# Retention attention and two MoE layers: the decay mask made on the chip, and a new order of the first loads

## Chip, cores and metric

The kernel runs on one core of a Trainium2 chip. The metric is the device time of one launch in microseconds (us), taken as the median of several runs. A profile is one execution more, with its own time. Five engines take part: PE (TensorE, matmuls), DVE (VectorE), ACT (ScalarE), SP (SyncE, which here only issues DMAs) and POOL (GpSimd, idle but for four constants at the start). PEld is the loading of weights into PE, which overlaps its matmuls.

## What is computed

```python
# attention: B, H, S, D = 2, 8, 768, 64
gamma = 1.0 - 2.0 ** (-5.0 - np.arange(H))
scale = 1.0 / np.sqrt(D)
for t in range(S):
    state = gamma * state + outer(k[:, :, t], v[:, :, t])
    y[:, :, t] = scale * (q[:, :, t] @ state)
# x = y as 1536 tokens x 512
h = x @ w_in;  x = (h * clip(h + 3, 0, 6) / 6) @ w_out        # layer 0, d_ff 2048
h = x @ w_in2; out = (h * tanh(softplus(h))) @ w_out2         # layer 1, d_ff 2048
```

Everything is float32 in and out. Matmuls of the two layers split each operand into a high and a low float32r part and take three passes (high by high, low by high, high by low).

## The kernel before

The attention is done in 12 units: six chunks of 128 positions for each of two batches; unit u is chunk u // 2 of batch u % 2. For a unit the names below are these. `qk` and `kv` are its two loads (512 and 516 KB). `sc` is the scores matmul (eight small fp32 matmuls, into one `wx` and one `wy` bank of PSUM). `m` are the two DVE multiplications of the scores by `mask`, which give `A` (L533). `kp` are eight ACT scalings of k (L524). `kv` on PE adds k by v to the running state in the bank `acc0` or `acc1` (L540 on), and `st` is ACT's copy of that state (L545). `qs` is DVE's scaling of q by a table, `qtab` (L529), in all units but the first two. `pv` is the output: `qs` by the state, then `A` by v. From its bank ACT writes `xh` (L580) and two quarters `q`/`qc` (L589), and DVE writes `xl` (L583). These are the inputs of layer 0.

Before the units, DVE zeroes a tile (L377) and PE multiplies zero by zero into `acc0` and `acc1` (`run_warm`, L380), which clears the two banks of the states. That is four fp32 matmuls of 256 columns.

The mask is a table of 128 by 1024 float32 (eight heads by 128 positions, for each of 128 key positions): the decay gamma to the power of the distance, times the scale, and zero above the diagonal. It is computed on the host and loaded as the third of the loads (L254).

The layers' weights come as `raw` words in 64 bits, of which ACT and DVE make float32 (`cvu`, `cvd`: L414 to L424) and then high and low parts (`wbh`, `wbl`, `tv`, `wdh`, `wdl`: L431, L433). An up-product `h` of layer 0 is 12 passes of 512 columns; `o` are the passes of the down-products.

The order of all this is made when the program is built. Every step is a task with an engine, an assumed duration and a rank, and `Plan.order` places the task that can start first, the lower rank first among equals. Ranks of the PE tasks of the beginning follow the string `EARLY`: s is `sc`, k is `kv`, b is `pv`, h is an up-product, o a down-product. The first loads are ranked by `LOADS`; what is not named there follows. `GATE` gives how long the up-products of the second layer are held back behind the first layer's last down-products. Each engine then runs its list in order, and so does SP's queue of DMAs. A load waits for its buffer (three each for `qk` and `kv`, two for `raw` and for `qtab`), and from the ninth on for the load issued eight places ahead of it to have landed, since eight semaphores serve the DMAs in turn.

Of the kernel before, what the change touches and what calls it, by code (L numbers as in the profile page):

```python
# [12 lines left out]
F32R = mybir.dt.float32r  # L13
# [3 lines left out]
ALU = mybir.AluOpType  # L17
PSUM = bass.MemoryType.PSUM

B, H, S, D = 2, 8, 768, 64  # L20
P = 128
# [4 lines left out]
NPAIR = H // 2  # L26
# [13 lines left out]
DMA512 = 1.28  # L40
MMR = 0.2266
MMH = 0.12
DVE1 = 0.686
# [3 lines left out]
SC, KV, PV = 0.9, 0.47, (0.9, 1.8)  # L47
TURN = 0.17
LEAD = (7.2, 6.1)
GATE = {'c': 8.0, 'w': 8.5, 'v': 8.0}  # L50
EARLY = "ssbsksbkskkbkksbbhkskbsbbksbokhoshbhshhoosbohohbohoohhhooo"
LOADS = "qk0 kv0 mask qk1 qk2 kv1 kv2 t1 kv3 qk3"
DLAT = 1.45
OUT = 4.0


# [27 lines left out]
class Plan:  # L84
# [3 lines left out]
    def add(self, nm, eng, dur, deps, bufs, emit, rank=None):  # L88
        t = Task(nm, eng, dur, deps, bufs, emit, rank)
        t.idx = len(self.tasks)  # L90
        self.tasks.append(t)
        for b in bufs:
            if not b.users:
                t.new.append(b)
                b.owner = t
            elif b.owner not in t.deps:
                t.deps.append(b.owner)
            b.users.append(t)
        for d in t.deps:
# [84 lines left out]
def body(ctx: ExitStack, tc: tile.TileContext, aps: dict, out: bass.AP):  # L184
# [39 lines left out]
    def wk(kind=None):  # L224
        if kind is None:
            turn[0] += 1
            kind = "xy"[turn[0] % 2]
        return buf("wk", [P, 512], "w" + kind)

    mask_b = buf("att", [P, 1024], "mask")  # L230
    qtab_b = {c: buf("att", [P, 512], "qtab") for c in range(1, NCH)}

    def load(nm, b, src, us, rank=None):
        return add(nm, "SP", us, [], [b],
                   lambda: nc.sync.dma_start(out=b.tile, in_=src), rank)  # L235
# [6 lines left out]
    def ld(u, what, rank=None):  # L242
        if what == "qk":
            ld_qk[u] = load(f"qk{u}", qk[u], aps["qk"][u], DMA512, rank=rank)
        else:
            ld_kv[u] = load(f"kv{u}", kv[u], aps["kv"][u], DMA512, rank=rank)

    tabs = aps["tabs"]
    lds = {}
    for n, what in enumerate(LOADS.split() + [f"{x}{u}" for u in range(NU) for x in ("qk", "kv")]  # L250
                             + [f"t{c}" for c in range(1, NCH)]):
        rank = -100 + n if n < len(LOADS.split()) else None
        if what == "mask":
            lds[what] = load("mask", mask_b, aps["mask"], DMA512, rank=rank)  # L254
        elif what[0] == "t":
            if what not in lds:
                c = int(what[1:])
                lds[what] = load(f"qtab{c}", qtab_b[c], tabs[:, (c - 1) * 512:c * 512], DMA512 / 2, rank=rank)
        elif what not in lds:
            ld(int(what[2:]), what[:2], rank)  # L260
            lds[what] = True
    ld_mask = lds["mask"]


    flow = []
# [40 lines left out]
    def source(i):  # L306
        layer, g, b, f = downs[i]
        if plain[layer, g]:
            return ("c", layer, f, b)
        if b == 0:  # L310
            return ("v", layer, f // 2, 4 if f % 2 else 3)
        return ("w", layer, f // 2, {(1, 0): 2, (1, 1): 4, (2, 0): 3, (2, 1): 7}[b, f % 2])
# [33 lines left out]
    hq = i = 0  # L346
    for c in EARLY:
        if c in "skb":
# [9 lines left out]
    while i < ND or hq < len(ups):  # L358
        nxt = ups[hq] if hq < len(ups) else None
        gate = 0.0  # L360
        if nxt and nxt[1] == 1:
            gate = max((done_at.get(b, 1e9) + GATE[nxt[0]]) for b in ((1, 2) if nxt[0] == "w" else (0,)))
        ready = up_end.get(source(i), 1e9) + LEAD[downs[i][0]] if i < ND else 1e9
# [9 lines left out]
            clock[0] = max(clock[0] + 0.05, min(ready, gate if nxt else 1e9))  # L373

    att_tasks = []
    zb = buf("fix", [P, 512], "t")
    z0 = add("zero", "DVE", DVE1, [], [zb], lambda: V.memset(zb.tile, 0.0), -99)  # L377
    kv_acc = [buf("acc", [P, 512], f"acc{b}") for b in range(B)]

    def run_warm():  # L380
        for a in kv_acc:
            for n in range(2):
                mm(a.tile[:, n * 256:n * 256 + 256], zb.tile[:, 0:P], zb.tile[:, 0:256], n == 0, True)
    t_warm = add("warm", "PE", 1.8, [z0], [zb] + kv_acc, run_warm, -99)

    wbase, wquart, wsum, wdown = {}, {}, {}, {}
    ld_w = [None]

# [113 lines left out]
    def unit(u):  # L502
        c, b = divmod(u, B)
# [4 lines left out]
        ps = [wk(), wk()]  # L508
# [6 lines left out]
        t_sc = add(f"sc{u}", "PE", SC, [ld_qk[u], pvs.get(u - BUFS["A"])], [qb] + ps, sc, pe_rank["sc", u])  # L515
# [11 lines left out]
        if c > 0:  # L527
            qsb = buf("att", [P, DM], "qs")
            t_qs = add(f"qs{u}", "DVE", DVE1, [ld_qk[u], lds[f"t{c}"]], [qb, qsb, qtab_b[c]], lambda: V.tensor_tensor(  # L529
                out=qsb.tile, in0=qb.tile[:, 0:512], in1=qtab_b[c].tile, op=ALU.mult))  # L530
        ab = buf("att", [P, 2, 512], "A")
        t_m = [add(f"m{u}_{i}", "DVE", DVE1, [t_sc, ld_mask], [ps[i], ab, mask_b],
                   lambda i=i: V.tensor_tensor(out=ab.tile[:, i, :], in0=ps[i].tile,  # L533
                                               in1=mask_b.tile[:, i * 512:(i + 1) * 512], op=ALU.mult))
               for i in range(2)]
# [39 lines left out]

        out_rank = pe_rank["pv", u] + PV[u >= B] + OUT

        def p3():
# [5 lines left out]
                                          op=ALU.subtract), out_rank + 0.7)  # L584
# [8 lines left out]
    for u in range(NU):  # L593
        unit(u)
# [295 lines left out]
def _tables():  # L890
    h = np.arange(H, dtype=np.float64)
    gam = 1.0 - 2.0 ** (-5.0 - h)
    scale = 1.0 / math.sqrt(D)
    i = np.arange(P)
    dif = i[None, :] - i[:, None]
    m = np.where(dif[:, None, :] >= 0, gam[None, :, None] ** np.maximum(dif, 0)[:, None, :], 0.0) * scale
    mask = m.reshape(P, NPAIR, 2, P).transpose(0, 2, 1, 3).reshape(P, 1024)
    gp = gam.reshape(NPAIR, 2)
    qt = [np.repeat((scale * gp[:, :, None] ** (c * P + i)).transpose(1, 0, 2)[:, None], 64, axis=1).reshape(P, 512)
          for c in range(1, NCH)]  # L900
    ktab = np.stack([gam[None, :] ** (-(u // B * P + i[:, None]).astype(np.float64)) for u in range(NU)])
    return mask.astype(np.float32), np.concatenate(qt, 1).astype(np.float32), ktab.astype(np.float32)


def _lay_w(w_in, w_out):
# [33 lines left out]
```

## Time and profile before

| | |
|---|---|
| median of 3 runs | 556.09 us (555.86 to 556.11) |
| the profiled execution, its own time | 556.31 us |
| its span, first to last recorded event | 554.5 us |
| PE busy | 544.5 us |
| DVE busy | 421.3 us |
| ACT busy | 289.7 us |
| bytes read and written by DMA | 51.2 MB |

The span is what the profile covers; 1.8 us of the execution lie around it. Busy time of PE includes the modelled ends of its matmuls, so short holes do not show in it. Busy shares are means over stages that have different limits: the first 25 us, in which the loads arrive one behind another, are not like the rest.

### The profile page before, as it was taken

The page shows a single profiled execution, that of the slowest core. Times are in us where ns is not written, and L with a number is a line of the kernel's source. Part 1 is how long each engine was busy: PE and PEld are TensorE (multiplying, and loading weights), DVE is VectorE, ACT ScalarE, POOL GpSimd, SP SyncE. Part 2 cuts the span into 40 slices and gives each one's busy share as a digit, 9 for nine tenths or more (in the row PEclk, how much of TensorE's full clock was granted, in tenths as well). Part 3 has the DMA queues.
Part 4 walks back from the last instruction along what each step waited for, and adds up shares of the span by engine and source line. Part 5 has one row for each costly group of instructions (what it writes and reads, how often), then busy time and mean ns, then how long its engine had stood idle before and what let it go on. Part 6 is the DMA issues. An engine that isn't in the chain of part 4 may idle for free.

```text
span 554.5 us, 8001 instructions
## 1 busy us (share of the span) xinstructions
PE 544.5 (98%) x3184; PEld 463.7 (84%) x3184; DVE 421.3 (76%) x651; ACT 289.7 (52%) x553; POOL 0.2 (0%) x4
## 2 busy tenths in 40 slices
PE   7899999999999999999999999999999999999997
PEld 6798888888889988888898888888888888988875
DVE  3799997599956996679999999899327985763243
ACT  4998645585625643455537665645433553442430
POOL 0000000000000000000000000000000000000000
PEclk9999999999999999999999999999999999999999
DMA  8986424003220233001222024224200240001003
GB/s 334 407 346 267 152 77 141 12 10 143 76 77 0 77 93 137 0 8 69 77 77 76 2 76 152 76 77 152 76 1 0 77 151 2 0 1 54 23 28 125
DMA packets 10981, 51.68 MB, mean 93 GB/s; under 512 B 1216, under 2 KB 1216, under 8 KB 7104
## 3 DMA queue, kind: packets, MB, share of 16 engines
q1 hardware_dynamic: 10944, 51.17, 25.8%
q8 instruction: 25, 0.41, 0.3%
q14 instruction: 12, 0.10, 0.1%
HBM read 48.02 MB, written 3.15 MB: 92 GB/s over the span
## 4 chain that ended last, share of the span: by engine, by line
PE 95%; DMA 3%; DVE 1%; SPq 0%; issue 0%
PE acc L216 51%; PE wx L216 24%; PE wy L216 20%; DMA qk<-in_qk_dram 3%; DVE sb L834 0%; SPq L235 0%; DVE g L745 0%
## 5 line engine op out<-in xcount | busy, mean ns | idle before, releaser
L216 PE MATMUL acc<-gh,wdh 128*128 128x512 f32 x192 | 74.9, 390 | 0.0
L216 PE MATMUL acc<-gh,wdl 128*128 128x512 f32 x192 | 74.8, 390 | 0.0
L216 PE MATMUL acc<-wdl,gh 128*128 128x512 f32 x192 | 74.8, 390 | 0.0
L216 PE MATMUL acc<-wdh,gh 128*128 128x512 f32 x192 | 74.8, 390 | 0.0
L216 PE MATMUL acc<-wdh,gl 128*128 128x512 f32 x192 | 74.7, 389 | 0.0
L216 PE MATMUL acc<-gl,wdh 128*128 128x512 f32 x192 | 74.7, 389 | 0.0
L781 DVE TENSOR_TENSOR gl<-g,gh 128x512 fp32r<-128x512 f32 x68 | 46.7, 687 | 25.7 <-ACT gh L779 21.1
L779 ACT CAST gh<-g 128x512 fp32r<-128x512 f32 x68 | 42.2, 621 | 30.3 <-PE acc L216 18.2
L745 DVE TENSOR_TENSOR g<-wy,g 128x256 f32<-128x256 f32 (+1 forms) x42 | 21.4, 509 | 28.6 <-PE wy L216 28.4
L216 PEld LDWEIGHTS acc<-gl,wdh 128*128 128x128 f32 x192 | 36.0, 188 | 7.6
L216 PEld LDWEIGHTS acc<-wdh,gl 128*128 128x128 f32 x192 | 36.0, 188 | 7.5
L216 PEld LDWEIGHTS acc<-gh,wdh 128*128 128x128 f32 x192 | 36.1, 188 | 7.3 <-issue 0.2
L216 PEld LDWEIGHTS acc<-wdh,gh 128*128 128x128 f32 x192 | 36.1, 188 | 7.2
L216 PEld LDWEIGHTS acc<-wdl,gh 128*128 128x128 f32 x192 | 36.1, 188 | 7.2
L216 PEld LDWEIGHTS acc<-gh,wdl 128*128 128x128 f32 x192 | 36.1, 188 | 7.0
L781 DVE TENSOR_TENSOR gl<-gs,gh 128x512 fp32r<-128x512 f32 x28 | 19.3, 688 | 22.7 <-ACT gh L779 16.9
L779 ACT CAST gh<-gs 128x512 fp32r<-128x512 f32 x28 | 17.4, 622 | 31.0 <-PE acc L216 30.9
L431 ACT CAST wdh<-cvd 128x512 fp32r<-128x512 f32 x32 | 19.7, 620 | 20.6 <-PE acc L216 16.3
L433 DVE TENSOR_TENSOR wdl<-cvd,wdh 128x512 fp32r<-128x512 f32 x32 | 21.9, 686 | 10.9 <-ACT wdh L431 10.5
L742 ACT COPY g<-wx 128x256 f32<-128x256 f32 (+1 forms) x42 | 18.5, 441 | 21.2 <-PE wx L216 20.9
L834 DVE SCALAR_TENSOR_TENSOR sb<-acc,sb 128x512 f32<-128x512 f32 x36 | 23.3, 685 | 4.5 <-PE acc L216 4.5
L431 ACT CAST wsh<-cvu 128x1024 fp32r<-128x1024 f32 x14 | 14.7, 1051 | 21.1 <-DVE cvu L477 21.0
(191 smaller groups left out, 1339.9 us busy)
## 6 DMA issues: line engine op xcount, KB each, us to landing
raw<-in_w_dram SPq DMA_DIRECT2D x30, 1024.0 KB, 4.8
kv<-in_kv_dram SPq DMA_DIRECT2D x12, 516.0 KB, 6.9
qk<-in_qk_dram SPq DMA_DIRECT2D x12, 512.0 KB, 7.4
out_dram<-sb SPq DMA_DIRECT2D x12, 256.0 KB, 2.1
raw<-in_w_dram SPq DMA_DIRECT2D x4, 512.0 KB, 10.0
qtab<-in_tabs_dram SPq DMA_DIRECT2D x5, 256.0 KB, 8.1
mask<-in_mask_dram SPq DMA_DIRECT2D x1, 512.0 KB, 6.1
```

The costliest lines, as they stand in the source:

```text
L216: nc.tensor.matmul(o, l, r, start=start, stop=stop, skip_group_check=True)
L431: lambda: A.copy(hb.tile[:, h0:h0 + n], cb.tile[:, c0:c0 + n]))
L433: return add(nm + "lo", "DVE", dve(n), [a], list(dict.fromkeys([cb, hb, lb])), lambda: V.tensor_tensor(out=lb.tile[:, l0:l0 + n], in0=cb.t ...
L742: lambda: A.copy(gb.tile[:, gc], ps.tile[:, pc]))
L745: return add(f"c{k}_{nm}", "DVE", dve(n), deps, [ps, gb], lambda: V.tensor_tensor(out=gb.tile[:, gc], in0=ps.tile[:, pc], in1=gb.tile[:, g ...
L779: a = add(f"hi{i}", "ACT", act(512), tg + [prev_split[0]], [gb, gh], lambda: A.copy(gh.tile, gb.tile))
L781: lambda: V.tensor_tensor(out=gl.tile, in0=gb.tile, in1=f32(gh.tile), op=ALU.subtract))
L834: lambda d=d, ac=ac: V.scalar_tensor_tensor(out=sb.tile[:, d, :], in0=ac.tile, scalar=sc, in1=sb.tile[:, d, :], op0=ALU.mult, op1=ALU.add) ...
```

## The change

The mask is no longer loaded. A table `fac` of eight rows (one for each head) is loaded instead: 128 columns of gamma to the power of minus the key position, and 1024 columns that hold, in row h, the scale times gamma to the power of the query position, in the 128 columns of head h, and zero elsewhere. A triangle `tri` of 128 by 128 ones and zeros is loaded too. Two fp32 matmuls of 512 columns multiply out the table into a `wx` and a `wy` bank, and two DVE multiplications by the triangle write the mask. The two loads are 37 and 66 KB, the mask was 524 KB.

The zeroing of the two banks becomes one float32r matmul of 512 columns for each.

`LOADS`, `EARLY` and `GATE` are new, and with them the order of tasks. The built programs differ in order on PE, ACT and DVE in the first part only: on PE the last difference is at row 351 of 2594, about the end of the first group of layer 0; behind it the rows are the same.

```diff
-GATE = {'c': 8.0, 'w': 8.5, 'v': 8.0}
-EARLY = "ssbsksbkskkbkksbbhkskbsbbksbokhoshbhshhoosbohohbohoohhhooo"
-LOADS = "qk0 kv0 mask qk1 qk2 kv1 kv2 t1 kv3 qk3"
+GATE = {'c': 7.0, 'w': 8.0, 'v': 8.0}
+EARLY = "sbsssbskkkkbksbshbkskkbkbbksbohoshbhhosohbsohhbohooohhhooo"
+LOADS = "tri fac qk0 qk1 kv0 qk2 qk3 kv1 kv2 kv3 t1"
...
-    zb = buf("fix", [P, 512], "t")
-    z0 = add("zero", "DVE", DVE1, [], [zb], lambda: V.memset(zb.tile, 0.0), -99)
+    zb = buf("fix", [P, 512], "t", F32R)
+    z0 = add("zero", "DVE", DVE1, [], [zb], lambda: V.memset(f32(zb.tile), 0.0), -99)
...
         for a in kv_acc:
-            for n in range(2):
-                mm(a.tile[:, n * 256:n * 256 + 256], zb.tile[:, 0:P], zb.tile[:, 0:256], n == 0, True)
-    t_warm = add("warm", "PE", 1.8, [z0], [zb] + kv_acc, run_warm, -99)
+            mm(a.tile, zb.tile[:, 0:P], zb.tile, True, True)
+    t_warm = add("warm", "PE", 0.9, [z0], [zb] + kv_acc, run_warm, -99)
+    ld_mask = []
+    for i in range(2):
+        o = wk("xy"[i])
+        t = add(f"mk{i}", "PE", 0.9, [lds["fac"], t_warm], [fac_b, o], lambda i=i, o=o: mm(
+            o.tile, fac_b.tile[:, 0:P], fac_b.tile[:, P + i * 512:P + i * 512 + 512], True, True), -98)
+        ld_mask.append(add(f"mask{i}", "DVE", DVE1, [t, lds["tri"]], [o, tri_b, mask_b], lambda i=i, o=o: V.tensor_tensor(
+            out=mask_b.tile[:, i * 512:(i + 1) * 512].rearrange("p (r i) -> p r i", r=NPAIR),
+            in0=o.tile.rearrange("p (r i) -> p r i", r=NPAIR),
+            in1=tri_b.tile.unsqueeze(1).broadcast_to([P, NPAIR, P]), op=ALU.mult), -98))
...
-        t_m = [add(f"m{u}_{i}", "DVE", DVE1, [t_sc, ld_mask], [ps[i], ab, mask_b],
+        t_m = [add(f"m{u}_{i}", "DVE", DVE1, [t_sc, ld_mask[i]], [ps[i], ab, mask_b],
```

What stands in a row at the three places where the order matters most is shown below, as the built programs have it. First SP's queue, from the first load on; `qk_72`, `qk_86`, `qk_88` and `qk_119` are the `qk` of units 0 to 3, `kv_76`, `kv_90` and `kv_92` the `kv` of units 0 to 2. Before:

```order
L235 DMA qk_72<-in_qk_dram 128x1024
L235 DMA kv_76<-in_kv_dram 128x1032
L235 DMA mask_84<-in_mask_dram 128x1024
L235 DMA qk_86<-in_qk_dram 128x1024
L235 DMA qk_88<-in_qk_dram 128x1024
L235 DMA kv_90<-in_kv_dram 128x1032
L235 DMA kv_92<-in_kv_dram 128x1032
L235 DMA qtab_94<-in_tabs_dram 128x512
L399 DMA raw_106<-in_w_dram 128x512
L235 DMA qtab_108<-in_tabs_dram 128x512
L235 DMA qk_119<-in_qk_dram 128x1024
L399 DMA raw_121<-in_w_dram 128x512
```

After (the `qk` of units 0 to 2 are `qk_82`, `qk_84` and `qk_90`, the `kv` are `kv_86`, `kv_92` and `kv_98`):

```order
L238 DMA fac_74<-in_fac_dram 8x1152
L238 DMA tri_76<-in_tri_dram 128x128
L238 DMA qk_82<-in_qk_dram 128x1024
L238 DMA qk_84<-in_qk_dram 128x1024
L238 DMA kv_86<-in_kv_dram 128x1032
L238 DMA qk_90<-in_qk_dram 128x1024
L238 DMA kv_92<-in_kv_dram 128x1032
L238 DMA kv_98<-in_kv_dram 128x1032
L238 DMA qtab_100<-in_tabs_dram 128x512
L412 DMA raw_103<-in_w_dram 128x512
L238 DMA qtab_115<-in_tabs_dram 128x512
L412 DMA raw_117<-in_w_dram 128x512
```

Two small loads stand ahead of all, the mask is gone, the `kv` of unit 0 has moved from second to third of the large loads, and a `raw` has moved ahead of the `qk` of unit 3. Further on `qk` 3, `qk` 4, `kv` 3 and `qk` 5 follow one another, and `kv` 4 comes behind a `raw`.

Second, ACT's list at its start. `kp_110`, `kp_174` and `kp_231` are the `kp` of units 0 to 2; `xch` and `qc` are the `xh` and the quarters of the first four units. Before:

```order
L524 ACTIVATE kp_110<-kv_76 128x64 x8
L545 COPY st_134<-acc_32_78 128x512
L580 CAST xch_162<-acc_39_150 128x4x128
L524 ACTIVATE kp_174<-kv_90 128x64 x8
L589 COPY qc_197<-acc_39_150 128x2x128
L589 COPY qc_209<-acc_39_150 128x2x128
L580 CAST xch_162<-acc_51_185 128x4x128
L524 ACTIVATE kp_231<-kv_92 128x64 x8
```

After:

```order
L537 ACTIVATE kp_138<-kv_86 128x64 x8
L593 CAST xch_167<-acc_43_147 128x4x128
L602 COPY qc_171<-acc_43_147 128x2x128
L602 COPY qc_181<-acc_43_147 128x2x128
L558 COPY st_196<-acc_34_78 128x512
L537 ACTIVATE kp_198<-kv_92 128x64 x8
L593 CAST xch_167<-acc_55_183 128x4x128
L427 ACTIVATE cvu_231<-raw_103 128x512
```

The state of unit 0 is copied behind the outputs of unit 0, no longer ahead of them.

Third, ACT's list some 45 us in, where `kp_646` and `kp_735` are those of units 8 and 9 before, `kp_658` and `kp_720` after, and `t` is the relu of the second up-product. Before:

```order
L524 ACTIVATE kp_646<-kv_501 128x64 x8
L589 COPY q_430<-acc_90_527 128x2x128
L589 COPY q_445<-acc_90_527 128x2x128
L580 CAST xah_406<-acc_97_591 128x4x128
L589 COPY q_430<-acc_97_591 128x2x128
L589 COPY q_445<-acc_97_591 128x2x128
L414 ACTIVATE cvu_701<-raw_549 128x1024
L666 ACTIVATE t_704<-wx_658,bias_70 128x512
L431 CAST wdh_707<-cvd_300 128x512
L580 CAST xbh_719<-acc_104_684 128x4x128
L524 ACTIVATE kp_735<-kv_564 128x64 x8
```

After:

```order
L537 ACTIVATE kp_658<-kv_516 128x64 x8
L558 COPY st_688<-acc_35_79 128x512
L602 COPY q_423<-acc_101_607 128x2x128
L602 COPY q_427<-acc_101_607 128x2x128
L427 ACTIVATE cvu_705<-raw_502 128x1024
L537 ACTIVATE kp_720<-kv_580 128x64 x8
L558 COPY st_750<-acc_34_78 128x512
L593 CAST xbh_761<-acc_108_668 128x4x128
```

The relu is gone from between the two: the second up-product, which PE did between `sc` and `pv` of units 9 and 8, now comes behind `sc` of unit 11, as do its helpers. The first up-product moved a little ahead, from behind `sc` 6 to between `pv` 4 and `kv` 4.

## Rows read from the trace of the kernel before

**Rows 1.** The page: busy time by engine (part 1), chain by engine (part 4).

```profile
PE 544.5 (98%) x3184; PEld 463.7 (84%) x3184; DVE 421.3 (76%) x651; ACT 289.7 (52%) x553; POOL 0.2 (0%) x4
...
PE 95%; DMA 3%; DVE 1%; SPq 0%; issue 0%
```

**Rows 2.** Busy time by stretch: stretch, its length, engines, granted PE clock, DMA share, GB/s.

```profile
20.00:30.00 10.00, 9.61 (x150) 8.82 (x151) 9.20 (x17) 8.45 (x28) 0.00 (x0) 1.00 1.03 414
30.00:40.00 10.00, 10.00 (x164) 9.05 (x164) 9.52 (x18) 9.98 (x35) 0.00 (x0) 1.00 0.87 328
```

**Rows 3.** Timeline, 5 to 24 us: start, duration, instruction, idle before and its releaser.

```profile
5.26 2.02 ACT L524 ACTIVATE kp<-kv 128x64 f32<-128x64 f32 x8 [3.25 <-DMA kv<-in_kv_dram]
...
7.83 0.69 DVE L533 TENSOR_TENSOR A<-wy,mask 128x512 f32<-128x512 f32 x1 [6.41 <-DMA mask<-in_mask_dram]
...
9.07 0.37 PE L216 MATMUL wy<-qk 64*128 64x128 f32 x1 [1.40 <-DMA qk<-in_qk_dram]
...
16.68 0.37 PE L216 MATMUL wy<-qk 64*128 64x128 f32 x1 [0.16 <-DMA qk<-in_qk_dram]
...
20.06 0.34 PE L216 MATMUL wy<-qk 64*128 64x128 f32 x1 [1.60 <-DMA qk<-in_qk_dram]
...
21.27 2.02 ACT L524 ACTIVATE kp<-kv 128x64 f32<-128x64 f32 x8 [0.89 <-DMA kv<-in_kv_dram]
...
23.87 0.34 PE L216 MATMUL wy<-qk 64*128 64x128 f32 x1 [0.19 <-DMA qk<-in_qk_dram]
```

**Rows 4.** Timeline, SP's first issues; last row: KB and landing of the first.

```profile
0.73 0.38 SPq L235 DMA_DIRECT2D qk<-in_qk_dram  x1
...
1.17 0.42 SPq L235 DMA_DIRECT2D kv<-in_kv_dram  x1
...
1.64 0.42 SPq L235 DMA_DIRECT2D mask<-in_mask_dram  x1
...
qk<-in_qk_dram SPq DMA_DIRECT2D x1, 512.0 KB, 3.3
```

**Rows 5.** Zeroing matmuls: timeline, weight loads (min/median/max ns), later loads (mean ns).

```profile
1.48 3.38 PE L216 MATMUL acc<-t 128*128 128x256 f32 x8 [1.48 <-DVE t L377]
...
L216 PEld LDWEIGHTS acc<-t x8: 257/337/337, 1.5 to 4.2; 128*128 128x128 f32 x8
...
L216 PEld LDWEIGHTS acc<-gl,wdh 128*128 128x128 f32 x192 | 36.0, 188 | 7.6
```

**Rows 6.** Timeline of ACT, 11.7 to 16.7 us.

```profile
11.78 2.02 ACT L524 ACTIVATE kp<-kv 128x64 f32<-128x64 f32 x8
...
13.70 0.62 ACT L589 COPY qc<-acc 128x256 f32<-128x256 f32 x2
...
14.22 0.59 ACT L580 CAST xch<-acc 128x512 fp32r<-128x512 f32 x1
...
14.70 2.03 ACT L524 ACTIVATE kp<-kv 128x64 f32<-128x64 f32 x8
```

**Rows 7.** Timeline of PE, 24.9 to 34 us: first row of each step.

```profile
24.96 1.09 PE L216 MATMUL acc<-qs,st 128*64 128x128 f32 x16
...
26.76 0.63 PE L216 MATMUL acc<-kv,kp 128*64 128x64 f32 x16
...
27.54 0.37 PE L216 MATMUL wx<-qk 64*128 64x128 f32 x1
...
28.63 0.50 PE L216 MATMUL wy<-xch,wbh 128*128 128x512 f32 x1
...
31.61 1.09 PE L216 MATMUL acc<-qs,st 128*64 128x128 f32 x16
...
33.41 0.63 PE L216 MATMUL acc<-kv,kp 128*64 128x64 f32 x16
...
33.98 0.37 PE L216 MATMUL wy<-qk 64*128 64x128 f32 x1
```

**Rows 8.** Timeline of SP: issue of the first 1 MB of weights.

```profile
36.49 0.33 SPq L399 DMA_DIRECT2D raw<-in_w_dram  x1
```

More of the change, by code (lines that the diff above doesn't have):

```diff
@@ L49 @@
 LEAD = (7.2, 6.1)
-GATE = {'c': 8.0, 'w': 8.5, 'v': 8.0}
-EARLY = "ssbsksbkskkbkksbbhkskbsbbksbokhoshbhshhoosbohohbohoohhhooo"
-LOADS = "qk0 kv0 mask qk1 qk2 kv1 kv2 t1 kv3 qk3"
+GATE = {'c': 7.0, 'w': 8.0, 'v': 8.0}
+EARLY = "sbsssbskkkkbksbshbkskkbkbbksbohoshbhhosohbsohhbohooohhhooo"
+LOADS = "tri fac qk0 qk1 kv0 qk2 qk3 kv1 kv2 kv3 t1"
 DLAT = 1.45
+FAC = P + 1024
 OUT = 4.0
@@ L230, in body @@
     mask_b = buf("att", [P, 1024], "mask")
+    fac_b = buf("att", [H, FAC], "fac")
+    tri_b = buf("att", [P, P], "tri")
     qtab_b = {c: buf("att", [P, 512], "qtab") for c in range(1, NCH)}
@@ L252, in body @@
         rank = -100 + n if n < len(LOADS.split()) else None
-        if what == "mask":
-            lds[what] = load("mask", mask_b, aps["mask"], DMA512, rank=rank)
+        if what == "fac":
+            lds[what] = load("fac", fac_b, aps["fac"], 0.2, rank=rank)
+        elif what == "tri":
+            lds[what] = load("tri", tri_b, aps["tri"], DMA512 / 8, rank=rank)
         elif what[0] == "t":
@@ L261, in body @@
             lds[what] = True
-    ld_mask = lds["mask"]
     flow = []
@@ L894, in _tables @@
     i = np.arange(P)
-    dif = i[None, :] - i[:, None]
-    m = np.where(dif[:, None, :] >= 0, gam[None, :, None] ** np.maximum(dif, 0)[:, None, :], 0.0) * scale
-    mask = m.reshape(P, NPAIR, 2, P).transpose(0, 2, 1, 3).reshape(P, 1024)
+    tri = (i[None, :] >= i[:, None]).astype(np.float64)
+    rows = np.arange(H)
+    right = np.zeros((H, 2, NPAIR, P))
+    right[rows, rows % 2, rows // 2] = scale * gam[:, None] ** i
+    fac = np.concatenate([gam[:, None] ** -i.astype(np.float64), right.reshape(H, 1024)], 1)
     gp = gam.reshape(NPAIR, 2)
@@ L901, in _tables @@
     ktab = np.stack([gam[None, :] ** (-(u // B * P + i[:, None]).astype(np.float64)) for u in range(NU)])
-    return mask.astype(np.float32), np.concatenate(qt, 1).astype(np.float32), ktab.astype(np.float32)
+    tabs = np.concatenate(qt, 1)
+    return tuple(x.astype(np.float32) for x in (fac, tri, tabs, ktab))
 def _lay_w(w_in, w_out):
@@ L918, in nat @@
         return x.reshape(B, H, NCH, P, D).transpose(2, 0, 3, 1, 4).reshape(NU, P, DM)
-    mask, tabs, ktab = _tables()
+    fac, tri, tabs, ktab = _tables()
     arrs = {
@@ L923 @@
         "kv": np.ascontiguousarray(np.concatenate([nat(k), nat(v), ktab], 2)),
-        "mask": mask,
+        "fac": fac,
+        "tri": tri,
         "tabs": tabs,
```

## The prediction, made before the changed kernel ran

> **What bounds the kernel now.** I read the page first [rows 1]: PE is busy for 98% of the span and makes up 95% of the chain that ended last, so the rest of the time is a little over 10 us of holes. Then I asked where PE waits. A few us lie at the very end and belong to the last stores; the change does not touch them. All but one of the others lie in the first 24 us, and the timeline names their releaser [rows 3]: PE starts `sc` 1 at 9.07, `sc` 3 at 16.68, `sc` 4 at 20.06 and `sc` 5 at 23.87, each time set free by a landed `qk`. From there to the last layer PE has no hole of note. So the kernel is bound by the loads until about 24 us and by PE after it, and **a change that only touches the beginning is worth what it brings forward at the point from which PE runs without holes**. The busy table shows a second thing [rows 2]: between 30 and 40 us ACT is busy for 9.98 of 10 us and DVE for 9.52. PE does not wait for them there, but they have next to nothing to spare.
>
> **Part 1, the loads.** The stream of loads is full: the DMA share is 1.03 at 414 GB/s between 20 and 30 us [rows 2]. I count places in it in units of 512 KB. Before, `qk` 0, `kv` 0, mask and `qk` 1 are places 1 to 4, `qk` 3 is 10, `qk` 4 is 12, `kv` 3 is 13 and `qk` 5 is 15. `qk` 0 landed at 0.73 + 3.3 = 4.03 [rows 4]; the others I take from whoever waited for them [rows 3]: `kv` 0 5.26, mask 7.83, `qk` 1 9.07, `qk` 3 16.68, `qk` 4 20.06, `kv` 3 21.27, `qk` 5 23.87. From place 12 to 15 that is 3.81 us for three, so 1.27 a place. Two steps are longer: 2.57 for the one place to the mask, and 3.38 for the two to `qk` 4, some 2.1 us more than 1.27 a place would give. I do not know their cause, and keep them where they are in time.
>
> After, fac and tri are issued first. An issue on SP takes 0.44 to 0.47 us, from 0.73 to 1.17 to 1.64 [rows 4], and the stream is nearly empty while they run; so `qk` 0 is issued at 1.64 and lands at 4.94, and **the whole stream starts 0.91 later**. Against that the mask is out, and loads have changed places. `qk` 3 stays tenth, since a `raw` went ahead of it: 16.68 + 0.91 = 17.6. `qk` 4 is 11th: 20.06 - 1.27 + 0.91 = 19.7. `kv` 3 is 12th: 20.9. `qk` 5 is 13th: 23.87 - 2.54 + 0.91 = 22.2. `kv` 0 is third and lands where the mask did, 7.83 + 0.91 = 8.7. The net gain of the removed mask is thus 0.36 us per load, and not 1.27; the new order adds for `qk` 5 and takes from `kv` 4 (15th, 24.8, not needed before 25.4).
>
> **Part 2, mask and zeroing on PE and DVE.** A load's fixed part is 3.3 - 1.27 = 2.0 us [rows 4], so fac, of 37 KB, is there at about 2.95 and tri at 3.5. The zeroing before was 1024 columns in fp32 and took 3.38 us [rows 5]. The granted clock reads 1.00 there, but a weight load took 337 ns where the same shape later takes 188 [rows 5], so this was the pace of the 1.2 GHz level, after an engine that had done nothing. The mask's two matmuls are 1024 columns of fp32 as well: 3.4 us at that pace, 1.7 at full pace, and I take the pace to change half way through. They end between 4.65 and 6.35, and `sc` 0 and `sc` 1 (1.09 each [rows 7]) by 8.5 at the latest. That costs nothing: the next on PE, `pv` 0, waits for `kv` 0 at 8.7. The two DVE multiplications (0.69 each, by the same shape at 7.83 [rows 3]) fall where DVE sat idle for 6.41 us. If that cover were gone they would cost 1.3. The zeroing itself shrinks by more than 2 us, and that is worth nothing by itself, since PE would only have waited for `qk` 0.
>
> The rows show a slow pace after idleness, under the zeroing, and the full pace later [rows 5]. The Trainium skill, "TensorE: Matmul & The Clock Gate", Part 1 on the clock gate, says that the slow level is the default and that sustained activity lifts it, which speaks against this change: it does less work at the start and leaves a hole before fac lands. No row here tells how long the slow level would last then. Were `sc` 0 and `sc` 1 slow too, they would end at 10.3 in place of 8.5, ACT's first `xh` would come 1.3 later, and of that about 0.3 would be left when ACT next waits (for `kv` 3); the sum below would be 0.3 us worse. By the trace's own pace it stays as it is.
>
> **Part 3, PE from `sc` 4 to `pv` 5.** `sc` 4 starts with its load at 19.7 and takes 1.09 (27.54 to 28.63 [rows 7]). `pv` 3 starts at 20.8, takes 1.80 (24.96 to 26.76), and its second half finds `kv` 3. `kp` 3 starts on ACT at 20.9 and lasts 1.92 (11.78 to 13.70 [rows 6]), so `kv` 3 on PE ends at about 23.4. Then `sc` 5 (load there since 22.2) to 24.5, `pv` 4 to 26.3, the up-product (2.98, 28.63 to 31.61) to 29.2, `kv` 4 (0.57, 33.41 to 33.98) to 29.8, `sc` 6 to 30.9. `pv` 5 starts at **30.9, where it started at 31.61 before, with the same work done: 0.7 us ahead.**
>
> **Part 4, units 6 to 9 without a filler.** Before, the second up-product ran between `sc` 9 and `pv` 8, and ACT gained 2.98 us on PE. Now PE goes through with 1.09 + 1.80 + 0.57 = 3.46 a unit, 10.4 for the three from `kv` 6 to `kv` 9. ACT needs for the same three units 3 x 1.92 of `kp`, 0.48 each for `st` and `xh` and 0.52 for the quarters [rows 6], less one `xh`, and two conversions of about 0.3 and 1.1: 11.1. It thus loses 0.7 to PE, and by my chain it stands 0.5 ahead of it at `kv` 6. So PE waits about **0.2** for `kp` 9. On SP the first 1 MB of weights, which waits for DVE to have used its buffer, is issued ahead of `kv` 8 and `qk` 9, at some 33 us and not 36.49 [rows 8]; these two queue behind its 2.5 us. `qk` 9 then lands at 40.4, and `sc` 9 could start at 40.1: up to **0.3** more, nothing if the stream is a little ahead. I take 0.1 for both on the forecast's side, since the first of them is small against the spread of the estimates, and keep 0.5 as the other end.
>
> **Part 5, the rest.** Behind `sc` 11 the same work is left, PE has the second up-product and more to fill its waits, and the order is the same from row 351 on. The new gates change no row. I set this at nothing, with PE's own work as the cover.
>
> **Sum.** 0.7 - 0.1 = 0.6 us less than the profiled execution, 556.31 - 0.6 = 555.7. That execution ran 0.2 above the median, so **555.5** as a median.
>
> **Rivals.**
> - *The mask's place in the stream shows in full.* The stream moves little in its first microsecond anyway, so the two small loads could slip in for less than 0.91, and the long step to the mask (2.57) may have belonged to something that the later start misses. Then loads gain between 1.3 and 2.2, of which ACT, which has little to spare, lets some 1.3 to 1.7 through: 554.6 on average. For it: a longer step at one place and not at others looks like an accident. Against it: the second long step came at 17 to 20 us, without the mask.
> - *ACT becomes the bound.* From `kp` 3 to `kp` 9 ACT has no pause in the new order, and there is no up-product to give it time. Every microsecond by which `kv` 3 lands later than 20.9, or by which ACT's conversions run over, goes to PE one for one in units 7 to 9. My gain is used up if ACT is late by 0.6 to 0.7; at 2.0 (both long steps falling ahead of `kv` 3 once more, or a slow PE at the start and a late `kv` 0) it is 557.5. For it: 9.98 of 10 us busy [rows 2], and ACT's first `kp` starts at 8.7, not 5.26. Against it: ACT sat idle for 0.89 before `kp` 3 [rows 3] and does so again by my chain.
> - *It does nothing*: the loads' later start eats the place that the mask frees, and PE waits as long elsewhere: 556.1. That lies in the forecast's own range.
>
> **How the numbers follow.** What a measurement of this kernel can tell from no change is about 0.2%, 1.1 us. I give my forecast and the case of nothing together 0.50 (554.98 to 557.2); the mask's place in full 0.35, nearly all of it beyond 1.1 us; ACT as the bound 0.15. So faster 0.35, same 0.50, slower 0.15. The forecast's own range is 554.9 to 556.4. For 8 in 10 it has to take in most of the first rival and a part of the second: 554.1 to 557.2.
>
> **What would show it.** In the profile after, `kp` 0 should start at about 8.7, `sc` 3 at 17.6, `sc` 4 at 19.7 and `kp` 3 at 20.9, set free by DMAs; `pv` 5 should start near 30.9; and PE should have waits of a few tenths at most, for ACT or a `qk`, between 36 and 50 us. Loads that land 1 us or more ahead of these times speak for the first rival. Waits of PE for `kp` in units 7 to 9 of together more than 1 us speak for the second. I would be wrong altogether if PE showed holes behind 55 us, in the part that I set at nothing.

## The result, and the profile after

The changed kernel takes 559.51 us (median of 6 runs, 558.22 to 560.30), the kernel before 556.10 (6 runs, 555.86 to 556.51). The ratio is 1.0055, with a 95% interval of 1.0045 to 1.0065: **slower by 0.55%**, where I had forecast 0.1% faster (555.5 us, with 554.1 to 557.2 for 8 in 10) and had given slower a chance of 0.15. The profiled execution took 559.88 us, with a span of 558.1.

The page, its busy times and the chain by engine, beside [rows 1]:

```profile
PE 548.4 (98%) x3182; PEld 464.8 (83%) x3182; DVE 423.0 (76%) x653; ACT 290.6 (52%) x553; POOL 0.2 (0%) x4
...
PE 92%; ACT 3%; DVE 3%; DMA 2%; issue 0%; DVEq 0%
```

The share that PE lost in the chain has gone to ACT and DVE. Where, the stretches tell (columns as in [rows 2]):

```profile
30.00:40.00 10.00, 9.34 (x163) 8.43 (x161) 9.43 (x18) 9.97 (x31) 0.00 (x0) 1.00 0.73 261
40.00:50.00 10.00, 8.50 (x156) 7.92 (x156) 8.51 (x16) 10.00 (x35) 0.00 (x0) 1.00 1.02 396
```

PE, busy for 10.00 of 10 us before between 30 and 40, now has 9.34, and 8.50 in the next ten. ACT is full in both. PE's waits by name, between 30 and 50 us (engine, line, releaser; us, times, longest); before, no wait of the PE engine itself is listed there:

```profile
PE wy L217 <- DMA qk<-in_qk_dram: 1.5, 2, 1.0
...
PE acc L217 <- ACT kp L537: 0.7, 1, 0.7
```

The name in the second row misleads: the matmul that waited there, the first of `pv` 6, does not read `kp` (part 4 below).

The start, from PE's timeline, beside [rows 5] and [rows 7]:

```profile
2.85 2.07 PE L217 MATMUL wx<-fac 8*128 8x512 f32 x2
4.72 1.91 PE L217 MATMUL wy<-fac 8*128 8x512 f32 x2
6.56 0.58 PE L217 MATMUL wy<-qk 64*128 64x128 f32 x1
...
11.65 0.37 PE L217 MATMUL wy<-qk 64*128 64x128 f32 x1
...
32.19 1.09 PE L217 MATMUL acc<-qs,st 128*64 128x128 f32 x16
```

The two mask matmuls take 1.87 and 1.84 us from start to start. `sc` 0 and `sc` 1 follow at 6.56 with records of 0.58 and 0.42 us where 0.37 and 0.27 are usual. Only `sc` 2, at 11.65, has the full pace. `pv` 5 starts at 32.19 (forecast 30.9, before 31.61).

To compare orders that do the same things in another sequence, I use a **lag**: how much later than in the kernel before the same work on PE is done, in the profiled executions. It is read at the start of `pv` 5, at the start of `pv` 10 (less 2.87 us where one up-product more lies behind PE by then, half of the 5.73 that two take behind `sc` 11 in the changed kernel), and behind 107 us, by DVE's `gl` rows, where it no longer changes in any run. After: **+0.6 at `pv` 5, +3.1 at `pv` 10, +3.6 from 107 us on.** So most of the loss is made in units 6 to 11.

### The profile page after: what moved, and what is told of

The parts are those of the page before. It is cut to its first block, busy times and chain, and to the rows that moved or that the text cites. A ratio compares the mean times of both kernels' runs of the same rounds, so it can differ in the third digit from the quotient of the medians.

```text
span 558.1 us, 8003 instructions
## 1 busy us (share of the span) xinstructions
PE 548.4 (98%) x3182; PEld 464.8 (83%) x3182; DVE 423.0 (76%) x653; ACT 290.6 (52%) x553; POOL 0.2 (0%) x4
## 3 DMA queue, kind: packets, MB, share of 16 engines
HBM read 47.60 MB, written 3.15 MB: 91 GB/s over the span
## 4 chain that ended last, share of the span: by engine, by line
PE 92%; ACT 3%; DVE 3%; DMA 2%; issue 0%; DVEq 0%
PE acc L217 48%; PE wx L217 25%; PE wy L217 20%; ACT kp L537 1%; DMA qk<-in_qk_dram 1%; DVE sb L847 0%; DVE A L546 0%; DMA fac<-in_fac_dram 0%; ACT xch L593 0%; ACT qc L602 0%; DVE xcl L596 0%; DVE xal L596 0%; ACT cvd L427 0%; DVE qs L542 0%; ACT q L602 0%
## 5 line engine op out<-in xcount | busy, mean ns | idle before, releaser
L792 ACT CAST gh<-gs 128x512 fp32r<-128x512 f32 x28 | 17.4, 623 | 31.0 <-PE acc L217 30.9
L755 ACT COPY g<-wx 128x256 f32<-128x256 f32 (+1 forms) x42 | 18.5, 441 | 21.2 <-PE wx L217 20.9
L444 ACT CAST wsh<-cvu 128x1024 fp32r<-128x1024 f32 x14 | 14.7, 1052 | 20.9 <-DVE cvu L490 20.9
```

What stands on the lines that cost most here:

```text
L444: lambda: A.copy(hb.tile[:, h0:h0 + n], cb.tile[:, c0:c0 + n]))
L755: lambda: A.copy(gb.tile[:, gc], ps.tile[:, pc]))
L792: a = add(f"hi{i}", "ACT", act(512), tg + [prev_split[0]], [gb, gh], lambda: A.copy(gh.tile, gb.tile))
```

## Experiments

All ratios are to runs of the kernel before, taken on the same chip at the same time, with 95% intervals. "a" in a diff is the changed kernel, "b" the kernel before.

| run | edit | median us | ratio | lag `pv` 5, `pv` 10, 107 us |
|---|---|---|---|---|
| after | | 559.51 | 1.0055 [1.0045, 1.0065] | +0.6, +3.1, +3.6 |
| e1 | a, long zeroing | 561.31 | 1.0072 [1.0045, 1.0098] | +3.0, +4.7, +5.2 |
| e2 | a, old tables | 559.34 | 1.0044 [1.0027, 1.0061] | (a third order) |
| e3 | a, old tables, long zeroing | 559.70 | 1.0053 [1.0037, 1.0070] | (a third order) |
| e4 | b, short zeroing | 556.69 | 1.0005 [0.9996, 1.0014] | -0.2, +0.1 |
| e5 | a, mask matmuls in bf16 | 558.69 | 1.0043 [1.0030, 1.0055] | +0.1, +1.8, +2.3 |
| e6 | b, two 8-row matmuls more | 563.35 | 1.0134 [1.0115, 1.0153] | (a third order) |
| e7 | b, two small loads ahead | 556.61 | 1.0008 [0.9999, 1.0017] | +0.4, +0.4 |
| e8 | a, fac and tri behind qk 0 | 558.86 | 1.0045 [1.0033, 1.0058] | +0.3, +1.9, +2.4 |
| e9 | a, all in b's order | 556.45 | 1.0002 [0.9994, 1.0011] | -0.5, -0.2, -0.1 |
| e10 | b, all in a's order | 560.12 | 1.0070 [1.0055, 1.0085] | -0.2, +2.0, +2.5 |
| e11 | e9, mask in bf16, fac behind qk 0 | 556.38 | 1.0006 [0.9994, 1.0019] | -1.0, -0.7, -0.7 |
| e12 | e6, in b's order | 559.04 | 1.0043 [1.0027, 1.0059] | +2.5, +2.8, +2.8 |
| e13 | a, b's order behind `pv` 5 | 557.24 | 1.0014 [1.0005, 1.0023] | -0.2, +0.5, +0.5 |
| e14 | a, b's order up to `pv` 5 | 559.01 | 1.0050 [1.0038, 1.0063] | -0.2, +3.1, +3.6 |
| e15 | a, up-product moved back | 559.99 | 1.0068 [1.0055, 1.0080] | +0.1, +2.0, +3.7 |
| e16 | a, 1 MB load moved back | 559.47 | 1.0053 [1.0039, 1.0067] | +0.9, +2.8, +3.3 |
| e17 | a, `kp` 5 and 6 moved ahead | 560.01 | 1.0052 [1.0039, 1.0066] | +1.1, +3.6, +4.1 |
| e18 | e15, e16 and e17 together | 560.64 | 1.0069 [1.0056, 1.0082] | -0.2, +2.5, +4.2 |

### First theories: the slow start, or the order

Theory A: the short zeroing leaves TensorE at its slow level. Theory B: the new order has no filler for ACT. The tables `EARLY`, `GATE` and `LOADS` and the zeroing can be set back one by one.

e1, the changed kernel with the old zeroing:

```diff
-            mm(a.tile, zb.tile[:, 0:P], zb.tile, True, True)
+            for n in range(2):
+                mm(a.tile[:, n * 256:n * 256 + 256], f32(zb.tile)[:, 0:P], f32(zb.tile)[:, 0:256], n == 0, True)
```

> The changed kernel, with one thing undone: the banks are cleared by the four fp32 matmuls of 256 columns of before again, everything else and the order as changed. Theory A (PE's slow pace at the start is what costs): the zeroing lasts from 1.5 to about 4.9 and the mask's matmuls, sc 0, sc 1 and pv 0 run at full pace; sc 2 starts near 10 and not at 11.65, kp 3 near 21 and not at 22.15, pv 5 near 31 and not at 32.2, and the kernel takes 556 to 557.5. Theory B (the new order without an up-product between the units costs, whatever the start): pv 5 comes earlier too, but PE still waits 2 us or more for kp and qk between 36 and 51 us, and the kernel takes 558 to 559.5.

e2, with the old tables (e3: and the old zeroing):

```diff
-EARLY = "sbsssbskkkkbksbshbkskkbkbbksbohoshbhhosohbsohhbohooohhhooo"
-LOADS = "tri fac qk0 qk1 kv0 qk2 qk3 kv1 kv2 kv3 t1"
+EARLY = "ssbsksbkskkbkksbbhkskbsbbksbokhoshbhshhoosbohohbohoohhhooo"
+LOADS = "tri fac qk0 kv0 qk1 qk2 kv1 kv2 t1 kv3 qk3"
```

> The mask made on the chip with the short zeroing, but EARLY and GATE of before, and the loads in the order of before with tri and fac put first and the mask left out. Theory A: sc 0 and sc 1 are still slow, ACT is still late, and the kernel is slower than before by 1 to 2.5 us (557 to 558.5). Theory B: the second up-product stands between sc 9 and pv 8 again and hides what ACT lacks; the kernel is within 0.7 us of before (555.4 to 556.8).

> As the run with the old order, and the zeroing of before as well: what is left of the change is the mask made on the chip in place of loaded. Theories A and B both say no loss here: 555.3 to 556.5. If it is 557 or more, making the mask on the chip costs by itself, through the 0.9 us by which the loads start later, and both theories lack something.

e4, the kernel before with the zeroing of the changed one:

> The kernel before, with one thing changed: two float32r matmuls of 512 columns clear the banks in place of four fp32 ones of 256. Theory A: PE starts sc 0 when its load lands, at 4.1 and not at 4.79, but sc 0 and the kv of unit 0 run at half pace, sc 1 perhaps too, and the kernel loses 0.3 to 1.5 us (556.4 to 557.6). Theory B: no loss, 555.6 to 556.4.

e4 runs at half pace until 13 us and is no slower than before. e1 is no faster than the changed kernel, but it does not test the theory: with the long zeroing too, the mask's matmuls, `sc` 0 and `sc` 1 ran at half pace, up to 12.3. What settles it for the new order is e10 below, at full pace from 8.18 on, 0.2 us ahead at `pv` 5, and slow all the same: **theory A fell**. e2 and e3 stayed slow with the old tables, so theory B seemed to fall too. That reading was wrong, and the programs' own order showed why: given the mask's tasks and their assumed 0.9 us each, the planner makes of the old tables a third order, with the second up-product behind `pv` 8 (not between `sc` 9 and `pv` 8) and `kv` 9 behind `sc` 11. The old tables do not give the old order.

### The mask's matmuls, or the loads

I took the mask as such for the cause next (theory C: its matmuls at half pace; theory D: the later loads). e5 splits each factor into three bf16 parts on the host, 48 rows in place of 8, one pass for each matmul:

```diff
-    fac_b = buf("att", [H, FAC], "fac")
+    fac_b = buf("att", [6 * H, FAC // 2], "fac", I32)
```

> The changed kernel, with the two mask matmuls in bf16: each factor of the table is split into three bf16 parts (48 rows in place of 8), so a matmul of 512 columns is one pass and not the passes of fp32. Same numbers to float32 accuracy, same order of instructions on all engines. Theory C (the two fp32 matmuls of the mask, 2.07 and 1.91 us on PE ahead of the first scores, are the loss): they take 0.9 us together, sc 0 starts when its load is there (about 4.9 and not 6.56), pv 0 starts at about 8.6 to 9.0 and not 10.28, pv 5 at about 31 and not 32.2; time 556.0 to 557.0. Theory D (the 0.9 us by which all loads come later is the loss): nothing changes, 559 to 560. Theory B (the order without a filler for ACT in units 6 to 9): nothing changes, 559 to 560.

e6 adds two matmuls of the mask's shape to the kernel before:

```diff
+    for i in range(2):
+        o = wk("xy"[i])
+        add(f"mk{i}", "PE", 0.9, [t_warm], [zb, o], lambda i=i, o=o: mm(
+            o.tile, zb.tile[0:H, 0:P], zb.tile[0:H, 0:512], True, True), -98)
```

> The kernel before, with two more fp32 matmuls behind the zeroing, of the mask matmuls' shape (8 rows, 128 by 512) but of zeros, into the same two banks; the mask is still loaded and nothing reads what they write. Theory C: they run at half pace from 4.9 to 8.8, sc 0 and all behind it is late as in the changed kernel with long zeroing, and the time is 558.5 to 560. Theory D: 556.4, no change, since no load moves. Theory B: 556.4.

e7 loads 8 by 1152 and 128 by 128 numbers ahead of `qk` 0, e8 has `LOADS` begin with "qk0 fac tri":

> The kernel before, with two small loads of the size of tri and fac issued ahead of all others (nothing reads them); the mask is still loaded. Theory D: all loads 0.9 later, as in the changed kernel, and no mask taken out: 558 to 560. Theory C: the loads' 0.9 us is mostly taken up by PE's waits in the first 24 us, at most 0.9 shows: 556.4 to 557.3. Theory B: the same as C.

> The changed kernel with the loads of fac and tri issued behind qk 0 and not ahead of it; fp32 mask matmuls as they are, same order on PE, ACT and DVE. Theory C: fac lands at about 4.2, the mask's matmuls run at half pace from 4.2 to 8.2, sc 0 behind them at 8.2 and so 1.6 later than 6.56: 559.5 to 561. Theory D: qk 0 lands at 4.0 and only the later loads are 0.9 late, a small part of the loss goes: 558.5 to 559.5. Theory B: nothing changes, 559 to 560.

e7 clears the loads (1.0008): **theory D fell**. In e5 the mask's matmuls take 0.4 us each, and e5 is still at 1.0043, so C explains at most some 0.7 us of the loss, and the intervals of e5 and of the changed kernel overlap (e8 gets about as much with the fp32 matmuls, by the place of two loads). e6 looked like a proof of C, but here too the planner had made another order, with the second up-product behind `sc` 10. The next four runs hold the order by hand.

### The order held by hand

A list of task names replaces the planner's last line; the dependencies stay as they are.

```diff
-        return sorted(out, key=lambda t: t.start)
+        return sorted(out, key=lambda t: PIN[f"{t.nm}@{t.eng}"])
```

> The changed kernel (mask from the table by two fp32 matmuls, fac and tri loaded first, short zeroing) with every engine's instructions and the loads held in the order of the kernel before, by a list of its tasks, so that no planner moves anything. The earlier runs with the old tables (e2, e3) did not have this: the planner, given the mask's tasks, made a third order of them. Theory F (the order is the loss: no filler for ACT in units 6 to 9): 555.5 to 556.6, no loss. Theory C (the start is the loss: the mask's matmuls and all up to pv 0 at half pace): 558 to 559.5. Both by halves: 557 to 558.

> The kernel before (mask loaded, long zeroing) with the instructions of PE, ACT and DVE held in the order of the changed kernel, and the loads in its order too, with qk 0, kv 0 and the mask ahead of them. Theory F: 558 to 559.5, with waits of PE for kp and for qk 9 and qk 10 between 33 and 50 us of 1.3 us or more. Theory C: 555.5 to 556.6. Both by halves: 557 to 558.

> The mask from the table in bf16 parts (one pass a matmul, same numbers to float32 accuracy), fac and tri loaded behind qk 0, short zeroing, all else in the order of the kernel before. Theory F: with the order back and the mask out of the loads, 555 to 556.2, as good as before or 1 us better. Theory C: the mask's matmuls are off the path here, but sc 0, sc 1 and pv 0 stay at half pace: 556.3 to 557.

> The kernel before with two more fp32 matmuls of the mask's shape (8 rows, of zeros, read by nothing) behind the zeroing, in the order of the kernel before; in e6 the same two made the planner move kv ahead of sc and the like. Theory F: 556.2 to 557.3, the 2 us at the start are taken up by PE's waits for loads up to 24 us, and e6's loss was its order. Theory C: 559 or more, as in e6.

**e9 and e10 settle it: the mask on the chip costs nothing by itself (1.0002), and the order alone costs at least as much as the whole change (1.0070).** e9 has the same slow start as the changed kernel. Its timeline of PE, the mask's matmuls and `pv` 5:

```profile
2.83 2.07 PE L270 MATMUL wx<-fac 8*128 8x512 f32 x2
4.70 1.91 PE L270 MATMUL wy<-fac 8*128 8x512 f32 x2
...
31.07 1.09 PE L270 MATMUL acc<-qs,st 128*64 128x128 f32 x16
```

And its two stretches, columns as in [rows 2]:

```profile
30.00:40.00 10.00, 9.88 (x169) 8.99 (x169) 9.68 (x19) 10.00 (x35) 0.00 (x0) 1.00 0.88 313
40.00:50.00 10.00, 9.86 (x143) 8.66 (x141) 9.52 (x18) 10.00 (x31) 0.00 (x0) 1.00 1.00 399
```

ACT is as full as in the changed kernel, but PE keeps 9.88 and 9.86. e12 shows that the cover at the start has an end: `sc` 0 at 6.5 costs nothing (e9), at 8.9 (behind the long zeroing and two such matmuls, with the mask still loaded) it costs 2.9 us in the median (one of six runs took 556.27); I had expected that to be covered too. e11 is 0.7 us ahead in its profiled execution but not in the median, so no version here beats the kernel before.

### Where in the order

The loss lies behind `pv` 5 if the lags are right. e13 takes the changed kernel's list up to `pv` 5 and the old list from there, e14 the reverse.

> The changed kernel, its order kept up to pv 5, and from there on the order of the kernel before (all engines and loads). Theory F1 (the loss lies behind pv 5, in units 6 to 11): 556.3 to 557.2. Theory F2 (the loss is made in the first 31 us and only shows later): 558.7 to 560, as the changed kernel.

> The other half: the changed kernel with the order of the kernel before up to pv 5 and its own order from there on. Theory F1: 558.3 to 560. Theory F2: 556 to 557.

**Behind `pv` 5 it is:** 1.0014 against 1.0050. The new order ahead of `pv` 5 costs at most some 0.1% (e13 against e9, with overlapping intervals), the one behind it some 0.4% (the changed kernel against e13). e14 is not the changed kernel's stretch as it was: `pv` 6 waits 1.64 us there, for DVE's `qs`, where the changed kernel has 0.66, and ACT pauses for 1.37, which it does not do there. Then single parts were moved back:

```diff
 sc9@PE
+h0_1_0@PE
...
 w0_1_00abs@ACT
+relu0_1_0@ACT
...
 T1v_0@DVE
+g0_1_0@DVE
```

> The changed kernel with one thing moved: the second up-product back to between sc 9 and pv 8, with its relu on ACT and its product on DVE at their places of before. Theory F1a (the missing filler leaves ACT behind): PE's waits for kp and qk in units 8 to 11 go, 557.5 to 558.5. Theory F1b (the 1 MB load ahead of kv 8 and qk 9 is what PE waits for): the load has its place still, qk 9 and qk 10 are waited for as before it, 559 to 560.

```diff
-w0_1_00@SP
 kv8@SP
 qk9@SP
+w0_1_00@SP
```

> The changed kernel with one thing moved: the first 1 MB load of weights back behind qk 9 on SP's queue; nothing else. Theory F1b: the waits for qk 9 and qk 10 (0.46 and 1.03 in the changed kernel) go, 557.8 to 558.6. Theory F1a: what the loads no longer hold back, ACT's kp does; 559 to 560.

```diff
-d0_0hi@ACT
-relu0_0_0@ACT
 kp5@ACT
+relu0_0_0@ACT
+d0_0hi@ACT
...
-hi0@ACT
-u0_0b1hi@ACT
 xh5@ACT
 kp6@ACT
+hi0@ACT
+u0_0b1hi@ACT
```

> The changed kernel with kp 5 ahead of the relu and wdh, and kp 6 ahead of gh and wbh on ACT, as before the change (and DVE's wdl and gl, which read what these write, behind the mask's multiplications of unit 7); PE and the loads as in the changed kernel. Theory F3 (ACT enters units 6 to 9 late because of these): PE's waits ahead of kv 5 and kv 6 (together 1.0) go, those behind become smaller: 557.8 to 558.8. Theory F4 (ACT's work for units 6 to 9 is too much wherever its parts stand): the waits only move, 559 to 560.

> As e17, and the second up-product back between sc 9 and pv 8 (as e15), and the 1 MB load back behind qk 9 (as e16). Theory F1 (these three together are what the order behind pv 5 costs): 556.8 to 557.6, as e13. If it stays above 558.3, the loss is in some other part of the order behind pv 5.

(In e17 two DVE tasks that read what these write, `wdl` and `gl`, are moved back too.)

None of the three helps the median, nor all together. Their traces show why. In the changed kernel, e10 and e16 PE's waits between `pv` 5 and `pv` 10 add up to 2.5, 2.2 and 1.8 us, within 0.1 of what the lag grows by in that stretch. **e16:** the wait for `qk` 9 is gone and that for `qk` 10 is 0.83, so the lag grows by 1.8 and not 2.5; but this execution came to `pv` 5 0.3 later, and the median does not show the gain. **e17:** `kv` 5 no longer waits for `kp` 5, but the wait at `pv` 6 is 1.33 and not 0.66. The relu, now behind `kp` 5, holds up DVE for 1.00 us, and with it the `qs` that `pv` 6 reads. **e15** does win by `pv` 10 (lag 2.0, not 3.1), and loses it again behind, since the place behind `sc` 11 that the up-product leaves is now a hole, where DVE is late with `xbl`. The two longest of PE's waits in e15 from 46 us on:

```profile
56.67 1.09 PE L270 MATMUL acc<-qs,st 128*64 128x128 f32 x16 [0.29 <-DVE xbl L649]
...
62.50 1.09 PE L270 MATMUL acc<-qs,st 128*64 128x128 f32 x16 [0.89 <-DVE xbl L649]
```

What stays open is which smallest set of moves behind `pv` 5 would do; the runs show only that the old stretch as a whole does, and that these three parts do not. One part was never moved back by itself, and by the traces it is the first to try: DVE's order in units 6 and 7 (part 4 below).

## Why the prediction was wrong, step by step

**Part 1, the loads: right, and of little use.** `kp` 0 was forecast at 8.7 and started at 8.37, set free by its DMA. But nobody waited for `qk` 3, `qk` 4 or `kv` 3: by then PE and ACT were later than the loads.

**Part 2: the costing at nothing was right, its pace was wrong.** e9 confirms that mask and zeroing hide behind PE's waits for loads. But I let the pace change half way through the mask's matmuls; it stayed at half until 11.65. The Trainium skill, "TensorE: Matmul & The Clock Gate", Part 1 on the clock gate, had it that the slow level is where the engine starts and that sustained activity lifts it. The trace agrees with it here, and I had held the trace of before against it. I priced slow `sc` 0 and 1 at 0.3 us for the sum (their end at 10.3 is 10.7 by my own terms, 6.35 and twice 2.18; they ended at 10.35). In the changed kernel they are worth more: see the last section.

**Part 3: 1.3 us off.** I had ACT idle 0.89 before `kp` 3 as in [rows 3], and so `kp` 3 at 20.9, set by its load. In the trace `kp` 3 starts at 22.15 straight behind a `st`: ACT had begun its chain at 11.77 with the first `xh`, behind a `pv` 0 that came late and slow, and had no such reserve. `pv` 5 came at 32.19, not 30.9. Of this 1.3 a part is chance: with the same order up to there it came at 31.42 in e13 and at 32.72 in e17.

**Part 4: the step that decided, 2.4 us off.** I took 0.1, with 0.5 as the other end. From lag +0.6 to +3.1 it cost 2.5. ACT's work was right: I gave it 11.1 us from `kp` 6 to `kp` 9, and it took 47.28 - 36.23 = 11.05. What failed is that the sum had no term for DVE, which I had read as busy for 9.52 of 10 us, and so none for the loads that wait for DVE. PE's rows in which the 2.5 us lie:

```profile
33.98 0.96 PE L217 MATMUL acc<-kv,kp 128*64 128x64 f32 x16
...
36.70 1.09 PE L217 MATMUL acc<-qs,st 128*64 128x128 f32 x16 [0.66 <-ACT kp L537]
...
43.05 0.34 PE L217 MATMUL wy<-qk 64*128 64x128 f32 x1 [0.46 <-DMA qk<-in_qk_dram]
...
47.60 0.34 PE L217 MATMUL wy<-qk 64*128 64x128 f32 x1 [1.03 <-DMA qk<-in_qk_dram]
```

`kv` 5 takes 0.96 and not 0.63, drawn out by `kp` 5: 0.33. With the three waits (`pv` 6, `qk` 9, `qk` 10) that is 2.48, all of the loss in this stretch. Behind the three stands DVE. Its `qs` of units 6 and 7, and SP's issues of `qk` 9 and `qk` 10:

```profile
35.87 0.68 DVE L542 TENSOR_TENSOR qs<-qk,qtab 128x512 f32<-128x512 f32 x1
...
39.20 0.68 DVE L542 TENSOR_TENSOR qs<-qk,qtab 128x512 f32<-128x512 f32 x1
```

```profile
36.58 0.33 SPq L238 DMA_DIRECT2D qk<-in_qk_dram  x1
...
39.91 0.33 SPq L238 DMA_DIRECT2D qk<-in_qk_dram  x1
```

The profile names ACT's `kp` at `pv` 6, but `pv` 6 reads `qs` 6, which ends at 36.55, and it starts 0.15 behind that, as it does within 0.01 in e13, e15, e16 and e17. The same `qs` is the last to read the buffer that `qk` 9 needs, and `qs` 7 that of `qk` 10: each load is issued 0.03 us behind it. Before, the two `qs` started at 33.73 and 37.58 and the loads were issued at 34.53 and 38.29. DVE has no pause from 31.59 to 42.9. The first up-product, moved ahead of `sc` 6, now has its conversions and its product on DVE ahead of unit 6's two multiplications by the mask; before, these came first (28.71 and 29.91). I had the first 1 MB of weights issued at some 33 and `qk` 9 landed at 40.4. The weights were issued at 35.41, when DVE had used their buffer, and `qk` 9 landed at 42.9. For `qk` 10 I had no term at all. The chain that ended last is on DVE from 31.59 on, up to `qs` 7, and goes on through the load to `sc` 10, which starts at 47.60:

```profile
39.28 0.60 DVE qs L542
39.88 0.03 DVE tv L446
39.91 7.56 DMA qk<-in_qk_dram
```

ACT comes next. Its `kp` 6 and 9 and the two waits around them:

```profile
30.03 0.37 ACT L602 COPY q<-acc 128x256 f32<-128x256 f32 x1 [0.76 <-DVE xal L596]
...
36.23 2.03 ACT L537 ACTIVATE kp<-kv 128x64 f32<-128x64 f32 x8
...
47.28 2.05 ACT L537 ACTIVATE kp<-kv 128x64 f32<-128x64 f32 x8
...
51.20 0.59 ACT L558 COPY st<-acc 128x512 f32<-128x512 f32 x1 [0.92 <-PE acc L217]
```

Between the first and the last of these rows ACT waits for nothing. But `kp` 9 ends at 49.33, and `kv` 9, which needs it, starts on PE at 50.49. From these rows I estimate that some 1.2 of the 2.5 us are owed to DVE and the loads alone, and that ACT would have held PE for most of the rest without them. In e13, with the old order from `pv` 5 on, the two `qs` start 3.1 and 6.1 us behind the start of `pv` 5, not 3.7 and 7.0. There PE waits for no load, and the lag grows by 0.7. No run moves DVE's tasks by themselves, so DVE's part is read from the traces and not tested.

PE's four units from `kv` 5 to `kv` 9 last 16.5 us (33.98 to 50.49), of which 4 x 3.46 = 13.8 is work. Before, with the up-product of 2.98 among them, they lasted 16.8 (33.41 to 50.19). **So the new order as a whole lost nearly all of the time of the up-product that it took out.** The up-product alone, put back in e15, makes them 18.2 (33.49 to 51.69): it covers 1.3 of its 2.98.

**Part 5: 0.5 us off.** I set the rest at nothing. The lag grows from 3.1 to 3.6 between `pv` 10 and 107 us, and I had named holes behind 55 us as the sign of being wrong altogether. PEld's waits there name DVE, in a place where three `o` follow `pv` 11 with no up-product between:

```profile
67.62 0.19 PEld L217 LDWEIGHTS acc<-gh,wdh 128*128 128x128 f32 x1 [0.48 <-DVE xbl L596]
```

**Sum.** 1.3 + 2.4 + 0.5 = 4.2 us lie between the 555.7 that I gave for the profiled execution and its 559.88. The time is on the side of the rival "ACT becomes the bound", and in the units that it named, but its sign did not come: that was waits for `kp` in units 7 to 9 of together more than 1 us. There are none; there PE waited 1.49 us for `qk` 9 and `qk` 10. ACT was full, as the rival said, and stood close behind. I had priced it at 557.5, since I let it in only through a late `kv` 3, and held against it an idle time of ACT that belonged to the order of before. No rival had DVE in it.

## What to carry to other kernels

Where the helper engines are full over a stretch, work out a new order for each of them, and as far as the loads that wait for the buffers that they free; I did it for ACT alone. Other work of the main engine in such a stretch covers the helpers' delays, and that cover is lost when the work is moved elsewhere. A reserve read from the trace of before belongs to the order of before: for a new order, run each helper's chain from its first instruction and not from the place of interest. A name in a list of waits is a first guess: check that the waiting instruction reads what is named. And where a planner sets the order, hold it by hand before judging any one edit: three runs here said the wrong thing because an added task or an old table made an order that neither kernel has.

## What was unexpected in the hardware

**The pace of TensorE at the start differs between executions of one and the same list.** Up to `pv` 5 e13, e17 and the changed kernel have the same instructions on PE in the same order. In PE's timeline of e13, the first `sc` behind `pv` 0 (the changed kernel's is at 11.65, above) and the start of `pv` 5:

```profile
10.93 0.37 PE L270 MATMUL wy<-qk 64*128 64x128 f32 x1
...
31.42 1.09 PE L270 MATMUL acc<-qs,st 128*64 128x128 f32 x16
```

And the same two rows of e17:

```profile
12.10 0.50 PE L270 MATMUL wy<-qk 64*128 64x128 f32 x1
...
32.72 1.09 PE L270 MATMUL acc<-qs,st 128*64 128x128 f32 x16
```

In e17 the first records of that `sc` are still slow (0.50), it starts 1.17 later, and `pv` 5 comes 1.30 later: in this order a slow start is passed on in full, not by the 0.3 that I had put on it. Whether this is why the runs of the changed kernel spread over 2.1 us is not shown: only one execution of each run has a trace, and those of before, which spread over 0.7 beside it, spread over 3.2 beside e9 to e12 (555.65 to 558.80).

**The granted clock can read 1.00 while matmuls run at half pace,** as it does in the changed kernel up to `pv` 0 at 10.28. In e6 the fall is seen: behind a zeroing at half pace the two 8-row matmuls ran at full pace (5.02 to 6.92), and then the granted clock fell to its lower level, 0.50 or 1.2 GHz. PE's busy time, granted clock, DMA share and GB/s by stretch:

```profile
5.00:8.00 3.00, 3.00 (x21) 1.00 1.01 411
8.00:9.00 1.00, 1.00 (x20) 0.60 1.01 411
9.00:11.00 2.00, 2.00 (x20) 0.50 1.01 415
11.00:12.00 1.00, 1.00 (x16) 0.70 1.05 408
12.00:15.00 3.00, 3.00 (x55) 1.00 1.03 371
```

An fp32 matmul of 512 columns took 1.87 us from start to start at half pace and 0.96 at full pace with only 8 rows in use. The few rows save nothing: in e12 the zeroing, 1024 columns with all 128 rows, took 3.71 us from start to start (1.48 to 5.19), and the two matmuls of 8 rows, 1024 columns as well, 3.70 (5.19 to 8.89).
